# Score masks on ScalarE and GpSimd, and input loads issued one by one, in a fused attention and SwiGLU kernel

## The chip, the cores and the metric

The kernel runs on one core of one Trainium2 chip. The metric is the device time of one execution in microseconds. Five engines work side by side: TensorE multiplies matrices and writes to PSUM, VectorE (DVE) and ScalarE (ACT) compute elementwise and can read PSUM, GpSimd (POOL) computes elementwise in SBUF, and SyncE (SP) issues transfers. Each works through its own list of instructions and waits on semaphores of the others.

## The reference

Everything is float32. First a gated linear recurrence per batch row and head, then a feed-forward block over all tokens:

```python
batch, n_heads, seq, head_dim = (4, 8, 768, 48)      # d_model 384, d_ff 1536
f = 1.0 / (1.0 + np.exp(-f_logit))
for t in range(S):
    state = f[:, :, t, :, None] * state + np.einsum('bhd,bhe->bhde', k[:, :, t], v[:, :, t])
    y[:, :, t] = np.einsum('bhd,bhde->bhe', q[:, :, t], state)
x = y.transpose(0, 2, 1, 3).reshape(B * S, H * D)
g = x @ w_gate
out = (g / (1.0 + np.exp(-g)) * (x @ w_val)) @ w_out
```

## The kernel before

The sequence is cut into six chunks of 128 tokens, c = 0 to 5. A unit is one chunk of one batch row, written (c,b) here; in the code its number is u = 4c + b. The recurrence over a chunk becomes matrix work. With running products of the gates, k and q are scaled (`kT`, `qT`), the scores are `kT` times `qT` over the chunk's tokens, and a mask keeps the scores whose key is not later than the query. From them and from the decayed state comes `y`, and the state is carried to the next chunk. The feed-forward block then takes a whole chunk of all four batch rows (512 tokens) at once.

`attention(u)` is a generator. Each `yield` ends a step, and a table of times (`times`, line 873) says at which point of the running feed-forward block each step is written into the program. The steps of a unit from chunk 2 on are, in order: the sigmoid of f on ScalarE (L584); VectorE's transpose of f into `gates` (L593); its transpose of k (L601); a backward scan (L605); the product `kT` (L559); for the turned units, those of chunks 3 and 4, a transpose of `kT` into the room of k and four transfers through DRAM (L620 to L624); a forward scan (L631); the transpose of q (L635); the product `qT`; the scores (L651) and, where not turned, a transpose of `kT` on TensorE (`kt`, L655); the emptying of both (L659 to L667); then the decay of the state, `y`, and the state's update.

Inputs of chunks 2 to 5 land in `rooms["f"]`, `rooms["k"]` and `rooms["q"]`, one room for each input, in four transfers of 32 tokens each on SP's queue (L438 to L442). A room can be filled again only when it has been transposed. `load_after(u)` (L744) does it once per unit: after the transpose of q it issues the loads of f, q and k for unit u + 1. v has rooms of its own and is loaded elsewhere.

The scores of a unit fill two PSUM banks of 128x512, one for even heads and one for odd. `SCORES` (L863) names when they are written and where they go: "b" is a pool of three small-work banks, "A" and "o" are banks of the feed-forward block. "A" has two banks, "o" two and "B" one, and a bank given out again waits until the earlier content has been read. In chunks 3 to 5 the units of b = 1 and 2 use "o" at the start of a triple and b = 3 uses "A" in the down phase; b = 0 uses "b" in chunk 3 and "A" after that. In chunk 2 the order is b, o, A, A.

The feed-forward block of a chunk (`mlp_fifteen`, L946) has four triples of fifteen products and then a down phase. A product is a pair of 128x256 matmuls. Within a triple its products go into the banks A, B, o, A, B, o, A, B, c, A, B, c, A, B, A ("c" also takes an "o" bank). All products named A of one triple share one bank, and those named B too, so each is copied to SBUF by ScalarE (L997) before the next one writes. VectorE joins the copies with sums (L893, L896), ScalarE applies Silu (L1008), and VectorE multiplies (L944). Products are counted from one: the third goes into "o", the fourth into A again, the seventh into A once more.

Nothing is reordered behind this plan. `in_order` (L759) ties the instructions of each engine, GpSimd and SP included, to the order in which they were written:

```python
    in_order(mark, (mybir.EngineType.PE, mybir.EngineType.DVE, mybir.EngineType.Activation, mybir.EngineType.Pool, mybir.EngineType.SP))
```

GpSimd's list in this part holds only small memsets of `gates` (L639), the transfers that carry `yT` into `xT` (L702, ten for a unit), and some output transfers. The functions that the change touches, and what calls them:

Of the kernel before, what the change touches and what calls it, by code (L numbers as in the profile page):

```python
# [14 lines left out]
ALU = mybir.AluOpType  # L15
# [275 lines left out]
def short_path(ctx, tc, ident, least, judge, q, k, v, f_logit, moe_w_gate, moe_w_val, moe_w_out, out):  # L291
# [9 lines left out]
    nc = tc.nc  # L301
    B, H, S, D = q.shape
    C = 128
    NCH = S // C
    HP = H // 2
# [10 lines left out]
    SQUARES = 2  # L316
# [16 lines left out]
    causal = const.tile([128, C], FP32, tag="causal", name="causal")  # L333
    nc.gpsimd.memset(causal, 1.0)
    nc.gpsimd.affine_select(out=causal, in_=causal, compare_op=ALU.is_ge, fill=0.0, base=0,
                            pattern=[[1, C]], channel_multiplier=-1)
# [27 lines left out]
    def pairs(t, off=0):  # L364
        return t[:, off:off + HP * N1].rearrange("p (a t) -> p a t", t=N1)
# [23 lines left out]
    units = [(b, c) for c in range(NCH) for b in range(B)]  # L389
# [16 lines left out]
    def v_of(u):  # L406
        return vs[u % (NV if units[u][1] < SQUARES else NV // 2)]

    def squares(nm):
        return rooms[nm][:, Q:Q + HP * RUN].rearrange("t (a i e) -> t a i e", a=HP, i=NI)[:, :, :, 0:Q]  # L410

    def split_squares(nm):
        return squares(nm).rearrange("t a (j i) e -> t a j i e", j=2)

    def in_turn(t):

        return t.rearrange("p a (t i) -> p a i t", i=NI)

    def parted(t):

        return t.rearrange("p (j a t i) -> p a j i t", j=2, a=HP, i=NI // 2)

    def load(u, what="fkqv"):
        b, c = units[u]
        rows = slice(c * C, (c + 1) * C)
        inputs = dict(f=f_logit, k=k, q=q, v=v)
        for nm in "fkqv" if c < SQUARES else "fqkv":
            src = inputs[nm]  # L430
            if nm not in what:
                continue
            if nm == "v":
                dst = v_of(u)
            elif c < SQUARES:
                dst = raw[nm][u % NRAW]
            else:
                for n in range(4):  # L438
                    at = Q * (1 - n % 2)
                    nc.sync.dma_start(  # L440
                        out=rooms[nm][Q * n:Q * (n + 1), at:at + HP * RUN].rearrange("t (a e) -> t a e", a=HP),
                        in_=src[b, n // 2::2, rows, :].rearrange("a (t i) d -> t a (i d)", i=NI))  # L442
                continue
            nc.sync.dma_start(out=dst[:, :, 0:D], in_=src[b, :, rows, :].rearrange("h t d -> t h d"))
# [88 lines left out]
    def bank(name):  # L533
        return banks[-1].tile([128, 512], FP32, tag="a", name=name)
# [10 lines left out]
    def attention(u):  # L545
        b, c = units[u]
# [29 lines left out]
        def transposed(name, src):  # L576
            p = bank(name)
            for a in range(HP):
                nc.tensor.transpose(p[:, a * C:(a + 1) * C],
                                    src[:, 2 * a:2 * a + 2, :].rearrange("t r d -> t (r d)"), ident)  # L580
            return p.rearrange("p (a t) -> p a t", t=C)
# [6 lines left out]
        else:  # L588
            p = transposed("fTp", fr)
            nc.scalar.activation(pairs(gate)[:, :, 1:N1], p, AF.Copy if u in ahead else AF.Sigmoid)  # L590
        yield
        if c >= SQUARES:
            nc.vector.transpose(in_turn(pairs(gate)[:, :, 1:N1]), squares("f"))  # L593
        yield

        kT = att.tile([128, HP, C], FP32, tag="kT", name="kT")
        qT = att.tile([128, HP, C], FP32, tag="qT", name="qT", bufs=2)
        kp, qp = kT, qT
        if c >= SQUARES:
            kp = qT.rearrange("p a t -> p (a t)")  # L600
            nc.vector.transpose(parted(kp), split_squares("k"))  # L601
        yield

        n = HP * N1
# [7 lines left out]
            qp = transposed("qTp", qr)  # L612
        multiply(kT, kp, pairs(tail, 2)[:, :, 0:C])
        yield
        turned = SQUARES < c < NCH - 1
        if turned:


            beside = rooms["k"][:, 0:HP * C].rearrange("p (i m) -> p i m", i=NI)
            nc.vector.transpose(beside.rearrange("p i (a e) -> p a i e", e=Q), kT.rearrange("p a (i e) -> p a i e", e=Q))  # L620
            turn = turn_pool.tile([Q, NI, HP, NI, Q], FP32, tag="turn", name="turn")
            for r in range(NI):
                nc.sync.dma_start(out=turn[:, :, :, r, :].rearrange("t i a e -> t (i a) e"),
                                  in_=beside[Q * r:Q * (r + 1)].rearrange("t i (a e) -> t (i a) e", e=Q))  # L624
        yield

        if c >= SQUARES:
# [5 lines left out]
        if c >= SQUARES:  # L633
            qp = tail[:, 0:HP * C]
            nc.vector.transpose(parted(qp), split_squares("q"))  # L635
            load_after(u)
        yield
        multiply(qT, qp, pairs(gate)[:, :, 1:N1])
        nc.gpsimd.memset(pairs(gate)[:, :, 0:1], 0.0)  # L639
        if 0 < c < SQUARES:  # L640
            load_after(u)
        if c < SQUARES:
            decay()
        yield
# [1 line left out]
        A = att.tile([128, 2, HP, C], FP32, tag="A", name="A")  # L646
        sc = [score_bank(u) for _ in range(2)]
# [4 lines left out]
        if c < NCH - 1 and not turned:  # L652
            p = bank("kt")
# [9 lines left out]
            else:  # L663
                nc.scalar.copy(kt, p)
        for par in range(2):
            nc.vector.tensor_tensor(A[:, par], sc[par].rearrange("p (a t) -> p a t", t=C),  # L666
                                    causal.unsqueeze(1).broadcast_to((128, HP, C)), ALU.mult)  # L667
        yield
        if c >= SQUARES:
            decay()  # L670
# [4 lines left out]
        if c and b < B - 1:  # L675
# [20 lines left out]
            for h in range(H):  # L696
                a, par = h // 2, h % 2
                f = h * D
                while f < (h + 1) * D:
# [3 lines left out]
                                                                       in_=yT[r:r + n, par, a // 2 * C:(a // 2 + 1) * C])  # L703
# [25 lines left out]
        if c < NCH - 1:  # L729
            p = bank("dS")  # L730
# [10 lines left out]
            nc.vector.tensor_tensor(states[b], decayed[:, :, 0:D], dS, ALU.add)  # L741
        yield

    def load_after(u):  # L744

        w = u + (1 if units[u][1] >= SQUARES else 2)
        if w < len(units) and (units[w][1] >= SQUARES) == (w == u + 1):
            load(w, "fkqv" if units[w][1] < SQUARES or w == SQUARES * B else "fkq")

    def attention_steps(c):  # L750

        runs = [attention(c * B + b) for b in range(B)]
        parts = [3, 6, 3, 3]
        order = sorted((2 * b + s, b, n) for b in range(B) for s, n in enumerate(parts))
        return [lambda b=b, n=n: [next(runs[b]) for _ in range(n)] for _, b, n in order]
# [125 lines left out]
    def score_bank(u):  # L881
        b, c = units[u]
        kind = SCORES[c][b][1] if c >= SQUARES else "b"
        if kind == "b":
            return bank("sc")
        return {"o": banks_o, "A": banks_a}[kind].tile([128, 512], FP32, tag=kind, name="sc")
# [314 lines left out]
    mark = traced[-1]  # L1201
    keep_warm(5)
    first = [attention(b) for b in range(B)]
    done = [0] * B

# [83 lines left out]
    for c in range(2, NCH):  # L1289
        for b in range(B):  # L1290
            run = attention(c * B + b)
            waiting += [((c - 2) * whole + t, lambda run=run: next(run)) for t in times(c)[b]]
# [107 lines left out]
```

## Time and profile before

Three runs gave 608.85, 607.35 and 607.47 us; the median is 607.47. The profiled execution:

| | |
|---|---|
| its own time | 607.02 us |
| span from first to last instruction | 605.3 us |
| VectorE masks, L666, all chunks | 48 of 684 ns, 30.9 us |
| of these from chunk 2 on | 32 of 685 ns, 20.6 us as the union of their times |
| ScalarE copies 128x512 from "A" to `c`, L997 | 40 of 584 ns |
| ScalarE table loads from 144 us on | 22 of 1283 ns |
| GpSimd transfers `xT<-yT`, L702 | 120 of 509 ns |
| GpSimd select 128x128 at the start, L335 | 284 ns |
| loads of f, k and q into the rooms | 64 transfers each, 96 KB, 2.2 to 2.5 us to landing |

Busy time by stretch, one for each fifteen-product block (chunks 1 to 5), in us:

| stretch | length | TensorE | VectorE | ScalarE | GpSimd |
|---|---|---|---|---|---|
| 144 to 241 | 97 | 96.06 | 84.70 | 49.81 | 15.64 |
| 241 to 337 | 96 | 95.24 | 81.58 | 48.89 | 16.53 |
| 337 to 430 | 93 | 93.00 | 77.40 | 47.92 | 16.52 |
| 430 to 521 | 91 | 91.00 | 67.00 | 43.67 | 16.41 |
| 521 to 605 | 84 | 79.29 | 44.86 | 33.90 | 1.10 |

A line of the timeline has the start in us, the duration in us, the engine with its line in the code, the operation, what it writes and reads, the size, how many instructions were merged, and in brackets the idle time of the engine before it with what ended it. In TensorE's waits the columns are the total in us, the number of times and the longest. PE is TensorE's matmuls and PEld its weight loads. The busy time of TensorE is modelled to the end of a pipelined matmul, so a loss is best seen in the starts: two products in a row start 0.86 us apart. The attention units of chunk c run beside the block of chunk c - 1; 521 to 605 has none.

### The profile page before, as it was taken

The page shows a single profiled execution, that of the slowest core. Times are in us where ns is not written, and L with a number is a line of the kernel's source. Part 1 is how long each engine was busy: PE and PEld are TensorE (multiplying, and loading weights), DVE is VectorE, ACT ScalarE, POOL GpSimd, SP SyncE. Part 2 cuts the span into 40 slices and gives each one's busy share as a digit, 9 for nine tenths or more (in the row PEclk, how much of TensorE's full clock was granted, in tenths as well). Part 3 has the DMA queues.
Part 4 walks back from the last instruction along what each step waited for, and adds up shares of the span by engine and source line. Part 5 has one row for each costly group of instructions (what it writes and reads, how often), then busy time and mean ns, then how long its engine had stood idle before and what let it go on. Part 6 is the DMA issues. An engine that isn't in the chain of part 4 may idle for free.

```text
span 605.3 us, 10815 instructions
## 1 busy us (share of the span) xinstructions
PE 592.4 (98%) x4028; PEld 487.7 (81%) x4028; DVE 476.5 (79%) x825; ACT 292.5 (48%) x557; POOL 70.4 (12%) x175
## 2 busy tenths in 40 slices
PE   7899999999999999999999999999999999999996
PEld 5744545667888899878899988899988899988896
DVE  7999895968999977989995978995878982566741
ACT  3567662314876521476632376742276740366600
POOL 1000000000030050030330030330030321000000
PEclk9999999999999999999999999999999999999999
DMA  9999371014231144443345243244231100100001
GB/s 198 242 251 357 136 198 27 7 27 138 80 82 48 45 117 104 104 112 96 73 112 127 78 117 95 53 120 110 74 105 52 28 7 9 53 1 1 1 1 56
DMA packets 110299, 55.11 MB, mean 91 GB/s; under 512 B 72992, under 2 KB 102688, under 8 KB 110240
## 3 DMA queue, kind: packets, MB, share of 16 engines
q1 hardware_dynamic: 103872, 47.67, 30.0%
q0 software_dynamic: 4352, 3.94, 1.9%
q10 hardware_dynamic: 2016, 2.75, 1.2%
q8 instruction: 33, 0.54, 0.4%
q14 instruction: 26, 0.21, 0.1%
HBM read 44.56 MB, written 6.82 MB: 85 GB/s over the span
## 4 chain that ended last, share of the span: by engine, by line
PE 87%; DVE 9%; issue 1%; ACT 1%; DMA 1%; SPq 0%; DVEq 0%; ACTq 0%
PE o L1091 19%; PE A L992 15%; PE B L992 12%; PE gate L790 5%; PE val L790 5%; PE c L992 5%; PE o L992 5%; PE sc L651 4%; PE o L1154 3%; PE o L813 3%; PE y L691 2%; PE y L712 2%; PE dS L732 2%; PE y L687 1%; DVE c L896 1%
## 5 line engine op out<-in xcount | busy, mean ns | idle before, releaser
L702 POOL DMA_DIRECT2D xT<-yT x120 | 60.1, 509 | 54.2 <-ACT yT L695 51.7
L992 PE MATMUL A<-xs,w_both 128*128 128x256 f32 x240 | 62.3, 382 | 0.8 <-ACT c L997 0.8
L1091 PE MATMUL o<-w_out,h 128*128 128x192 f32 x360 | 62.0, 327 | 0.5 <-DVE h L944 0.5
L1091 PEld LDWEIGHTS o<-w_out,h 128*128 128x128 f32 x360 | 58.7, 190 | 1.7 <-DVE h L944 0.8
L997 ACT COPY c<-A 128x512 f32<-128x512 f32 x40 | 23.3, 584 | 57.7 <-PE A L992 57.7
L997 ACT COPY aside<-A 128x512 f32<-128x512 f32 x60 | 35.1, 585 | 33.1 <-PE A L992 33.0
L992 PEld LDWEIGHTS A<-xs,w_both 128*128 128x128 f32 x240 | 44.8, 190 | 7.7 <-ACT c L997 1.2
L893 DVE TENSOR_TENSOR c<-c,aside 128x512 f32<-128x512 f32 x60 | 41.1, 685 | 12.4 <-ACT aside L997 10.8
L944 DVE TENSOR_TENSOR h<-h,c 128x256 f32<-128x256 f32 x100 | 40.5, 413 | 7.8 <-ACT h L1008 7.6
L666 DVE TENSOR_TENSOR A<-sc,causal 128x512 f32<-128x512 f32 x48 | 30.9, 684 | 17.6 <-PE sc L651 17.6
L1008 ACT ACTIVATE h<-c 128x256 f32<-128x256 f32 x100 | 39.2, 416 | 7.8 <-DVE c L893 5.6
L896 DVE TENSOR_TENSOR c<-c,aside 128x512 f32<-128x512 f32 x60 | 40.9, 682 | 2.5 <-ACT aside L997 2.5
L1091 PE MATMUL o<-ws,h 128*128 128x192 f32 x240 | 41.5, 328 | 0.2 <-DVE A L666 0.2
L992 PE MATMUL B<-xs,w_both 128*128 128x256 f32 x160 | 41.3, 380 | 0.1
L992 PE MATMUL A<-xs,extra 128*128 128x256 f32 x160 | 41.3, 380 | 0.0
L992 PE MATMUL c<-xT,w_both 128*128 128x256 f32 x160 | 41.2, 380 | 0.1
L992 PE MATMUL B<-xT,extra 128*128 128x256 f32 x160 | 41.1, 379 | 0.0
L639 POOL MEMSET gates<- 128x4 f32 x24 | 3.0, 123 | 326.3 <-DVE qT L559 321.2
L997 ACT COPY aside<-B 128x512 f32<-128x512 f32 x60 | 35.1, 586 | 9.6 <-PE B L992 7.0
L1091 PEld LDWEIGHTS o<-ws,h 128*128 128x128 f32 x240 | 39.1, 190 | 0.8 <-DVE A L666 0.4
L893 DVE TENSOR_TENSOR c<-c,o 128x384 f32<-128x384 f32 x15 | 8.3, 552 | 36.0 <-PE o L1091 36.0
L896 DVE TENSOR_TENSOR c<-o,c 128x512 f32<-128x512 f32 x40 | 27.3, 684 | 10.6 <-ACT h L1008 6.2
(142 smaller groups left out, 1199.2 us busy)
## 6 DMA issues: line engine op xcount, KB each, us to landing
fsquares<-in_f_logit_dram SPq DMA_DIRECT2D x64, 96.0 KB, 2.5
qsquares<-in_q_dram SPq DMA_DIRECT2D x64, 96.0 KB, 2.2
ksquares<-in_k_dram SPq DMA_DIRECT2D x64, 96.0 KB, 2.2
v<-in_v_dram SPq DMA_DIRECT2D x24, 192.0 KB, 2.8
w<-in_moe_w_gate_dram SPq DMA_DIRECT2D x6, 768.0 KB, 6.3
w<-in_moe_w_val_dram SPq DMA_DIRECT2D x6, 768.0 KB, 6.0
w<-in_moe_w_out_dram SPq DMA_DIRECT2D x6, 768.0 KB, 5.0
out_dram<-ob ACTq DMA_DIRECT2D x14, 192.0 KB, 2.5
```

Of the source, the lines that this page charges most:

```text
L651: nc.tensor.matmul(sc[par][:, a * C:(a + 1) * C], lhsT=kT[r, a, :], rhs=qT[r, a, :], start=True, stop=True)
L666: nc.vector.tensor_tensor(A[:, par], sc[par].rearrange("p (a t) -> p a t", t=C), causal.unsqueeze(1).broadcast_to((128, HP, C)), ALU.mult)
L702: (nc.gpsimd if c >= SQUARES else nc.sync).dma_start(out=xT[c][f % 128:f % 128 + n, f // 128, b * C:(b + 1) * C], in_=yT[r:r + n, par, a / ...
L790: nc.tensor.matmul(p, lhsT=w[:, j, i, :], rhs=xT[c][:, i, :], start=(i == 0), stop=(i == KT - 1))
L813: nc.tensor.matmul(p, lhsT=hidden_tile(h, n // 2)[:, n % 2 * 2 + b // 2, b % 2 * C:(b % 2 + 1) * C], rhs=w_out[:, j, :], start=(n == 0), s ...
L893: nc.vector.tensor_tensor(dst, a, b, ALU.add)
L896: nc.vector.tensor_tensor(dst, a, b, ALU.subtract)
L944: lagging.append(lambda: f(*args))
L992: nc.tensor.matmul(p[name][:, n, :], lhsT=weights_of[a][:, n, j, :], rhs=tokens[b], start=fresh and n == 0, stop=True, skip_group_check=True)
L997: nc.scalar.copy(t, p[name])
L1008: nc.scalar.activation(dst, src[:, 0, :], AF.Silu)
L1091: nc.tensor.matmul(p[:, n, :], lhsT=lhsTs[j][:, n * C:(n + 1) * C], rhs=rhs[:, j, :], start=first and j == order[0] and n == 0, stop=j == ...
```

## The change

For chunks 2 to 5 the masking of the scores is split. ScalarE copies each score bank into `A`, and GpSimd then sets to zero in place what lies on the wrong side of the diagonal. The steps stay where they were written. Chunks 0 and 1 keep the multiplication by `causal` on VectorE.

`load_after` now takes the names of what to load for the next unit and is called three times: for f behind f's transpose, for k behind k's transpose (in turned units behind the four transfers out of k's room), and for q behind q's transpose. The loads of chunk 1 keep their rule, written out in place.

```diff
@@ -591,14 +591,18 @@
         yield
         if c >= SQUARES:
             nc.vector.transpose(in_turn(pairs(gate)[:, :, 1:N1]), squares("f"))
-        yield
-
+            load_after(u, "f")
+        yield
+
+        turned = SQUARES < c < NCH - 1
         kT = att.tile([128, HP, C], FP32, tag="kT", name="kT")
         qT = att.tile([128, HP, C], FP32, tag="qT", name="qT", bufs=2)
         kp, qp = kT, qT
         if c >= SQUARES:
             kp = qT.rearrange("p a t -> p (a t)")
             nc.vector.transpose(parted(kp), split_squares("k"))
+            if not turned:
+                load_after(u, "k")
         yield
 
         n = HP * N1
@@ -612,7 +616,6 @@
             qp = transposed("qTp", qr)
         multiply(kT, kp, pairs(tail, 2)[:, :, 0:C])
         yield
-        turned = SQUARES < c < NCH - 1
         if turned:
 
 
@@ -622,6 +625,7 @@
             for r in range(NI):
                 nc.sync.dma_start(out=turn[:, :, :, r, :].rearrange("t i a e -> t (i a) e"),
                                   in_=beside[Q * r:Q * (r + 1)].rearrange("t i (a e) -> t (i a) e", e=Q))
+            load_after(u, "k")
         yield
 
         if c >= SQUARES:
@@ -633,12 +637,12 @@
         if c >= SQUARES:
             qp = tail[:, 0:HP * C]
             nc.vector.transpose(parted(qp), split_squares("q"))
-            load_after(u)
+            load_after(u, "qv" if c < SQUARES else "q")
         yield
         multiply(qT, qp, pairs(gate)[:, :, 1:N1])
         nc.gpsimd.memset(pairs(gate)[:, :, 0:1], 0.0)
-        if 0 < c < SQUARES:
-            load_after(u)
+        if 0 < c < SQUARES and u + 2 < SQUARES * B:
+            load(u + 2)
         if c < SQUARES:
             decay()
         yield
@@ -663,8 +667,13 @@
             else:
                 nc.scalar.copy(kt, p)
         for par in range(2):
-            nc.vector.tensor_tensor(A[:, par], sc[par].rearrange("p (a t) -> p a t", t=C),
-                                    causal.unsqueeze(1).broadcast_to((128, HP, C)), ALU.mult)
+            p = sc[par].rearrange("p (a t) -> p a t", t=C)
+            if c >= SQUARES:
+                nc.scalar.copy(A[:, par], p)
+                nc.gpsimd.affine_select(out=A[:, par], in_=A[:, par], compare_op=ALU.is_ge, fill=0.0, base=0,
+                                        pattern=[[0, HP], [1, C]], channel_multiplier=-1)
+            else:
+                nc.vector.tensor_tensor(A[:, par], p, causal.unsqueeze(1).broadcast_to((128, HP, C)), ALU.mult)
         yield
         if c >= SQUARES:
             decay()
@@ -741,11 +750,10 @@
             nc.vector.tensor_tensor(states[b], decayed[:, :, 0:D], dS, ALU.add)
         yield
 
-    def load_after(u):
-
-        w = u + (1 if units[u][1] >= SQUARES else 2)
-        if w < len(units) and (units[w][1] >= SQUARES) == (w == u + 1):
-            load(w, "fkqv" if units[w][1] < SQUARES or w == SQUARES * B else "fkq")
+    def load_after(u, what):
+
+        if u + 1 < len(units):
+            load(u + 1, what)
 
     def attention_steps(c):
 
```

In program order ScalarE's new copies follow directly on these instructions, up to the next one of the list:

| unit | ScalarE's order around the two new copies |
|---|---|
| (2,0) | `c<-A`, `c<-B`, `kt`, **both**, table load, Silu, `c<-A` |
| (2,1) | `c<-A`, `kt`, **both**, `c<-B`, table load, Silu, `c<-A` |
| (2,2), (2,3) | `yT` twice, `kt`, **both** |
| (3,0) | `c<-A`, `c<-B`, `c<-A`, **both**, `aside<-B` |
| (3,1), (3,2), (4,1), (4,2), (5,1), (5,2) | `yT` twice, `c<-A`, **both**, `c<-B`, table load, Silu, `c<-A` |
| (3,3), (4,3), (5,3) | `yT` twice, **both**, `diagonal` |
| (4,0), (5,0) | `xT`, **both**, output transfers |

## Prediction

> **What bounds the kernel now.** I read the totals and the chain of waits first, then TensorE's waits, then the order of time around every place where the change puts an instruction. Chunks count from 0 here, as in the code, so the third chunk is c=2, and (c,b) is one unit. The page and TensorE's waits:
>
> ```profile
> span 605.3 us, 10815 instructions
> PE 592.4 (98%) x4028; PEld 487.7 (81%) x4028; DVE 476.5 (79%) x825; ACT 292.5 (48%) x557; POOL 70.4 (12%) x175
> ...
> PE 87%; DVE 9%; issue 1%; ACT 1%; DMA 1%; SPq 0%; DVEq 0%; ACTq 0%
> ```
>
> ```profile
> PE A L992 <- ACT c L997: 0.8, 1, 0.8
> ...
> PE o L1091 <- DVE h L944: 0.5, 1, 0.5
> ...
> PE o L1091 <- DVE A L666: 0.2, 1, 0.2
> ```
>
> TensorE sets the end: 98% busy, 87% of the chain. VectorE's 79% is no bound by itself. Every edit acts after 144 us, where the first fifteen-product block starts. There TensorE starts a product every 0.86 us, and a longer step between two starts is lost time. I find five: the second product of a triple starts at 189.99 instead of 189.70 (0.29), another at 196.38 (0.25), the down phase at 205.97 (0.70), 223.03 (0.18) and 262.46 (0.93), in all 2.35 us. From 265 us to the end there is none. So the change can win little more than 2.35 us, 0.4%, however much VectorE is relieved, while anything that holds TensorE costs in full.
>
> The last of these losses belongs to the loads:
>
> ```profile
> 257.75 1.16 PE L651 MATMUL sc<-qT,kT 48*128 48x128 f32 x16
> ...
> 258.94 1.29 DVE L666 TENSOR_TENSOR A<-sc,causal 128x512 f32<-128x512 f32 x2 [0.51 <-PE sc L651]
> ...
> 259.46 1.28 ACT L584 ACT_TABLE_LOAD   x1 [3.70 <-DMA fsquares<-in_f_logit_dram]
> ...
> 262.46 1.13 PE L992 MATMUL A<-xs,w_both 128*128 128x256 f32 x4 [0.76 <-ACT c L997]
> ```
>
> ScalarE stood 3.70 us before the sigmoid of (3,2) because f's squares had not landed; the copy of the first product queued behind it, and the next product into that bank waited.
>
> **What the Trainium skill says.** "PSUM — Partial Sum Buffer", section "Engine vs sequencer instructions": ScalarE, VectorE and GpSimd queues are strict FIFO, and matmuls start in program order. The trace agrees: the copy at 262 us stood behind a sigmoid that it does not need. "GPSIMD Engine Reference", section 3.1: a one-input loop of 512 elements took 769 ns; no trace here shows a select of that size. "SBUF — State Buffer", section "SBUF: two separate sides": a VectorE instruction with two SBUF inputs and a GpSimd instruction that reads SBUF exclude each other for a whole instruction. Before, GpSimd reads no SBUF but for two selects at the start, so the trace does not show it.
>
> **The change part by part.** The plan of positions and banks is untouched; only who empties the score banks changes, and each engine keeps its written order.
>
> *VectorE loses* the two masks of each of 16 units: 32 x 0.685 = 21.9 us busy, 1.29 us per unit. From 265 us on TensorE loses nothing to VectorE, so there it brings nothing. The losses at 189.99, 196.38 and 205.97 hang on VectorE's backlog (weight sums of 1.35 us at 187 and 194 among them). But the masks of (2,1) lie at 175.36, and VectorE then works up to TensorE's third product (starts at 178.61, 0.11 after that ended at 178.50). What is gained earlier is waited away there. I take 0; bound -1.25 us.
>
> *ScalarE gains* two copies of 128x512 from PSUM per unit. The row of the same shape has 584 ns, and copies in a row start 0.48 to 0.49 apart. What counts is what stands behind them:
>
> ```profile
> 353.38 1.29 DVE L666 TENSOR_TENSOR A<-sc,causal 128x512 f32<-128x512 f32 x2 [2.85 <-PE sc L651]
> ...
> 354.44 0.59 ACT L997 COPY c<-A 128x512 f32<-128x512 f32 x1 [1.80 <-PE A L992]
> ...
> 355.11 1.03 PE L992 MATMUL o<-xT,w_both 128*128 128x256 f32 x4
> 355.31 0.59 ACT L997 COPY c<-B 128x512 f32<-128x512 f32 x1 [0.28 <-PE B L992]
> ...
> 355.91 1.28 ACT L1008 ACT_TABLE_LOAD   x1
> ```
>
> (4,1) has its scores in both "o" banks, and the third product takes the first of them again. VectorE freed it at 354.07, long before 355.11. In the new order the copies stand behind `c<-A`, although the scores lie ready from 353.35: first copy 354.93 to 355.52, TensorE 0.05 later (as at 262.41/262.46), so the third product starts at 355.57: 0.46 us lost. After such a stop the following product comes 0.10 late as well (262.46 to 263.43 is 0.97 instead of 0.86; at 189.99 the same). The later bank waits still hold: `c<-A` of the fourth product would end at 358.71 instead of 358.10, and the seventh product, itself now after 359, needs it. So 0.56 us per unit. The same sum at (3,2), (4,2), (5,1), (5,2) (`c<-A` ends 291.27, 384.57, 447.88, 476.96; third product 291.34, 384.64, 447.96, 477.04) gives 0.46 to 0.47 each. Five units: 2.8 us.
>
> (2,1) is such a unit too, with the `kt` copy in front:
>
> ```profile
> 176.81 0.59 ACT L997 COPY c<-A 128x512 f32<-128x512 f32 x1 [2.55 <-PE A L992]
> ...
> 177.30 0.59 ACT L664 COPY kt<-kt 128x512 f32<-128x512 f32 x1
> ...
> 177.48 1.03 PE L992 MATMUL o<-xT,w_both 128*128 128x256 f32 x4
> ```
>
> `kt` ends at 177.89, the first score copy at 178.38, so the third product starts at 178.43 instead of 177.48: 0.95 + 0.10 = 1.05 us.
>
> (2,0) has its scores in other banks, but ScalarE is full there: copy, copy, `kt`, table load, Silu, and `c<-A` ends at 163.94 with the seventh product starting at 163.99 on that very copy. Two copies ahead of the table load push all by 2 x 0.49: 0.97 us.
>
> (2,3): the scores hold both "A" banks and the down phase's next sum takes the first at once:
>
> ```profile
> 222.28 1.29 DVE L666 TENSOR_TENSOR A<-sc,causal 128x512 f32<-128x512 f32 x2 [2.20 <-PE sc L651]
> 222.93 0.59 ACT L664 COPY kt<-kt 128x512 f32<-128x512 f32 x1 [1.80 <-PE kt L655]
> 223.03 1.44 PEld L1091 LDWEIGHTS o<-ws,h 128*128 128x128 f32 x9 [0.43 <-DVE A L666]
> ```
>
> Today VectorE frees it at 222.97. After: `kt` to 223.51, first copy 223.41 to 224.00, TensorE at 224.05: 1.02 us. The remaining units, (2,2), (3,0), (3,3), (4,0), (4,3), (5,0), (5,3), cost nothing: ScalarE waits around them and their banks come round 4 us later or more; (3,0) has the least cover, the copy for the eighth product ending at 248.21 against 248.54.
>
> *GpSimd gains* 32 selects. The select of 128x128 took 284 ns. Four times its elements at the same fixed part is about 0.54 us with the memset rows' slope (205 ns for 128 elements, 123 for 4), and 1.14 at most; I take the page's 0.77. They queue behind a unit's ten `xT` DMAs (5 us). Tightest is (2,2): DMAs until about 215.5, two selects to 217.1, the `y` matmul reading A at 219.61. It would wait only above 2 us per select. Price 0. If selects and VectorE's two-input instructions block each other, VectorE loses up to 2 x 0.77 per unit and gets 1.29 back; where it has no slack, between (2,1)'s selects at about 180 and 190, that is up to +1.5 us. I take 0, range 0 to 1.5.
>
> *Loads.* f is fetched behind f's own transpose, k behind its own (turned units: behind the turn DMAs that read k's room), q last. For (3,2) the f DMAs go out at about 244.7, when its predecessor's transpose ends, instead of 255.16; with 2.5 us to land they are there by 250, before ScalarE is ready at 255.77. On SP the `kt` load of (3,0) moves behind them, to about 246.6, needed at 257.20: covered. The 3.70 us wait goes, and TensorE's 0.93 with its 0.10. But then (3,1), whose score copies stand there, meets the "o" bank wait like the others, 0.46 and 0.10. Net -0.47 us. Elsewhere no load is late for TensorE: 0.
>
> **Sum.** 0.97 + 1.05 + 1.02 + 2.80 - 0.47 = +5.4 us. On the profiled execution's own 607.02 us (span 605.3 and 1.7 around it) that is 612.4 us, +0.9%. The median of the three runs is 607.47, 0.45 above the profiled one; on it the sum would be 612.9. I keep 612.4.
>
> **Rivals.**
> 1. *Bank waits and ScalarE's queue, as summed*: 612.4. For: each place has its start times; against: VectorE's slack may repay some. Chance 0.55.
> 2. *VectorE's relief repays in chunk 2*: the stops at 190, 196 and 206 (1.24 and three times 0.10) disappear: 610.9. For: VectorE is 98% busy from 180 to 210 us (29.4 of 30); against: the wait at 178.61. Chance 0.13.
> 3. *GpSimd and VectorE block each other*: +1.5 around 190, 613.9, and more if it recurs. Chance 0.14.
> 4. *The other side: VectorE's backlog is the true limit.* All five losses with their restarts go (2.35 + 0.4) and none of the new waits appears: 604.3. It decides if the copies release the "o" banks before the third product, that is, if they ran in ScalarE's 1.8 us gap ahead of `c<-A`. The written order speaks against it. Chance 0.09.
> 5. *Gains and waits cancel*: half the new waits (2.9) against the losses: 607 to 608. Chance 0.09. If f's load does not come in time, (3,1) keeps its loss: 612.9, inside case 1.
>
> **How the numbers follow.** About 0.3%, 1.8 us, can be told from no change. Slower: cases 1 to 3, 0.82; same: case 5, 0.09; faster: case 4, 0.09. The range takes cases 1 to 3 with their unknown costs, from 1.24 repaid plus a few copies that hide better, 609.5, to 1.5 of blocking plus second-order delays, 614.8.
>
> **What would show it.** TensorE's waits should name ScalarE's score copy ahead of `o` products in the third product of (2,1), (3,1), (3,2), (4,1), (4,2), (5,1) and (5,2), 0.4 to 0.5 us each and twice that at the first; a wait of about 1 us in the down phase of (2,3) and one near 165 us; none on f's DMA. VectorE's durations of two-input rows should stay at 0.68. I am wrong if the third products start on time, if VectorE's rows grow, or if a `y` matmul waits for GpSimd.

## The result, and the profile after

The changed kernel took 612.07 us (median of six runs, 612.0 to 612.94) against 607.42 for the kernel before (six runs, 607.22 to 608.85). The ratio is 1.0073, interval 1.006 to 1.0086: slower by 0.7%. The profiled execution took 612.16 us, its span 610.4, against 607.02 and 605.3. The forecast was 612.4, a sum of 5.4 us on top of the profiled execution before.

The page of the changed kernel, with its totals and its chain of waits:

```profile
span 610.4 us, 10917 instructions
...
PE 594.6 (97%) x4028; PEld 488.1 (80%) x4028; DVE 461.9 (76%) x793; ACT 308.2 (50%) x589; POOL 97.3 (16%) x207
...
PE 89%; DVE 7%; ACT 2%; issue 1%; ACTq 0%; DVEq 0%
```

VectorE did become lighter: 476.5 to 461.9 us. ScalarE gained 15.7 us and GpSimd 26.9, and both still idle half of the time or more. Read by busy shares, the change relieves the second busiest engine with two idle ones. Yet the end came 5 us later. TensorE's waits in the changed kernel (total in us, times, longest) say why:

```profile
PE o L1000 <- ACT A L672: 2.6, 7, 0.8
...
PE o L1099 <- ACT A L672: 1.2, 1, 1.2
PE A L1000 <- ACT c L1005: 0.9, 1, 0.9
...
PE o L1099 <- DVE h L952: 0.5, 1, 0.5
```

The first two rows are new. ScalarE's score copy (L672) now holds TensorE eight times: seven third products and one sum of the down phase. The third row looks like the one shown of before, `PE A L992 <- ACT c L997` with 0.8, and is another event: there it was the product at 262 us behind f's load, now it is the seventh product of (2,0) near 165 us, whose copy is late because two score copies were put ahead of it. A figure of this list is the idle time before the instruction and is not the loss itself. So I set the starts of all matmuls of both traces side by side; the loss is what the distance grows by. It is 0.12 us at 144 us, where the first block begins. It then grows by 0.975 us in (2,0), by 1.06 in (2,1), by 1.03 in (2,3), and by 0.57 at each of six more, and shrinks by 1.13 at the wait for f. The last of TensorE's products starts 5.43 us late, so 5.31 come from the region of the change. (The span grew by 5.1: what follows the last product was about 0.3 shorter. Single executions of one kernel differ by more than that, so it is the shifts of the starts, and not the totals, that are set against the terms of the prediction.)

One of the six, in the timeline of the changed kernel:

```profile
357.61 0.59 ACT L1005 COPY c<-A 128x512 f32<-128x512 f32 x1 [2.16 <-PE A L1000]
358.09 1.08 ACT L672 COPY A<-sc 128x512 f32<-128x512 f32 x2
358.73 0.73 PEld L1000 LDWEIGHTS o<-xT,w_both 128*128 128x128 f32 x4 [0.70 <-ACT A L672]
...
359.05 0.62 ACT L1005 COPY c<-B 128x512 f32<-128x512 f32 x1
```

ScalarE stood idle for 2.16 us, and for the last 1.1 of them the scores lay ready (their matmuls end at 356.51). It waited for the first product, because the copy `c<-A` is written ahead of the score copies, and only then emptied the "o" bank. The third product starts 0.05 us after the first of the two copies ends (358.09 + 0.59 = 358.68).

### The profile page after: what moved, and what is told of

The parts are those of the page before. It is cut to its first block, busy times and chain, and to the rows that moved or that the text cites. A ratio compares the mean times of both kernels' runs of the same rounds, so it can differ in the third digit from the quotient of the medians.

```text
span 610.4 us, 10917 instructions
## 1 busy us (share of the span) xinstructions
PE 594.6 (97%) x4028; PEld 488.1 (80%) x4028; DVE 461.9 (76%) x793; ACT 308.2 (50%) x589; POOL 97.3 (16%) x207
## 4 chain that ended last, share of the span: by engine, by line
PE 89%; DVE 7%; ACT 2%; issue 1%; ACTq 0%; DVEq 0%
PE o L1099 19%; PE A L1000 16%; PE B L1000 12%; PE o L1000 6%; PE c L1000 5%; PE gate L798 5%; PE val L798 5%; PE sc L655 4%; PE o L1162 3%; PE o L821 3%; PE y L700 2%; PE y L721 2%; PE dS L741 2%; PE y L696 1%; PE kt L659 1%
## 5 line engine op out<-in xcount | busy, mean ns | idle before, releaser
L1000 PEld LDWEIGHTS A<-xs,extra 128*128 128x128 f32 x160 | 30.3, 190 | 5.4 <-ACT c L1005 1.3
```

Of the source, the lines that this page charges most:

```text
L1000: nc.tensor.matmul(p[name][:, n, :], lhsT=weights_of[a][:, n, j, :], rhs=tokens[b], start=fresh and n == 0, stop=True, skip_group_check=True)
```

## The experiments

Each expectation was written before its kernel ran. All ratios are to the kernel before, run on the same chip.

**The loads alone.** The masks stay VectorE's multiplication; the loads are split as in the change. This edit and the next are shown against the changed kernel, shortened (`...`).

```diff
         for par in range(2):
-            p = sc[par].rearrange("p (a t) -> p a t", t=C)
-            if c >= SQUARES:
-                nc.scalar.copy(A[:, par], p)
-                nc.gpsimd.affine_select(out=A[:, par], in_=A[:, par], ...)
-            else:
-                nc.vector.tensor_tensor(A[:, par], p, ...causal..., ALU.mult)
+            nc.vector.tensor_tensor(A[:, par], sc[par]..., ...causal..., ALU.mult)
```

> The masks stay on VectorE, the loads are issued one by one as in the change. If ScalarE's queue and the bank waits are the whole cost, none of them is here and only the late f of (3,2) goes: TensorE starts its products after 265 us 1.13 us earlier than before (0.93 for the wait, 0.20 for the two restarts behind it), so about 606.3 us, 0.998 of before. If the reordered loads themselves cost something (the kt loads now stand behind f's loads on SP), it is no faster than before, 607.4 or more.

Measured: 605.93 us (605.62 to 608.17), ratio 0.9978, interval 0.9968 to 0.9987. TensorE's starts shift at one place only, by -0.93 and two restarts of -0.10, where f was late; its last product moves by -1.11. ScalarE's waits for f's loads, before:

```profile
ACT fsquares L584 <- DMA fsquares<-in_f_logit_dram: 10.4, 3, 5.2
...
ACT L584 <- DMA fsquares<-in_f_logit_dram: 4.1, 2, 3.7
```

and in the changed kernel:

```profile
ACT fsquares L584 <- DMA fsquares<-in_f_logit_dram: 4.0, 1, 4.0
```

Five waits of 14.5 us in all became one of 4.0 (3.8 with the loads alone), which lies at 138 us, ahead of the region of the change. Of the 10.5 us only one wait, the 3.7 of (3,2), had held TensorE. So the loads are the good part of the change, and they are worth 1.1 us.

**The masks alone.** The loads are issued as before (the remarks behind `#` are not in the code).

```diff
-            load_after(u, "f")       # behind f's transpose
-                load_after(u, "k")   # behind k's transpose, or the turn
-            load_after(u, "q")
+            load_after(u)            # all three behind q's transpose
```

> The masks move to ScalarE and GpSimd, the loads stay as before. My theory: the same losses at (2,0), (2,1), (2,3) and the five o-bank units (0.98, 1.06, 1.03 and 5 x 0.57), but at (3,1) ScalarE is late by f's wait and the score copy comes behind that: the third product waits from 260.67 to about 262.94, 2.37 us with its restart, in place of the 1.13 us of before. Sum +7.1 us: 614.6, 1.0117 of before. If the split loads and the masks were independent, this would be after plus 1.13 us, 613.2. If VectorE's relief pays for anything, less than either.

Measured: 615.8 us (614.61 to 616.93), ratio 1.0147, interval 1.0128 to 1.0166; TensorE's last product 8.37 us late. The new stops are those of the change, with two differences. First, the third product of (3,1) loses 2.97 us, not the 2.27 expected. The timeline of this kernel:

```profile
263.21 1.28 ACT L584 ACT_TABLE_LOAD   x1 [4.05 <-DMA fsquares<-in_f_logit_dram]
...
265.56 0.60 ACT L1002 COPY c<-A 128x512 f32<-128x512 f32 x1
...
266.03 1.10 ACT L668 COPY A<-sc 128x512 f32<-128x512 f32 x2
...
266.70 1.13 PE L997 MATMUL o<-xT,w_both 128*128 128x256 f32 x4 [2.81 <-ACT A L668]
```

The sigmoid of the next unit waits for f, and behind it stand `c<-A`, the score copies, and with them TensorE. A load that did not stand ahead of the mask in the kernel before now does, in ScalarE's queue. The extra 0.7 has two halves. f's transfers begin to issue 3.39 us later than in the kernel before (258.55 against 255.16), while TensorE was 3.04 late by then; and from there to ScalarE's table load for the sigmoid it takes 4.66 us instead of 4.30. The four took 3.31 us to issue instead of 2.05; why, stays open. The two parts of the change are not independent: splitting the loads is worth 1.1 us by itself and 3.1 (8.37 against 5.31) where the masks are on ScalarE.

Second, there are two stops that neither the kernel before nor the changed one has, 0.14 us at 276 and 0.47 at 371. What stands out ahead of the larger one is an instruction seven microseconds earlier:

```profile
364.75 1.23 POOL L669 TENSOR_SCALAR_AFFINE_SELECT A<-A 128x512 f32<-128x512 f32 x2
...
364.88 1.64 DVE L898 TENSOR_TENSOR c<-c,aside 128x512 f32<-128x512 f32 x1 [0.54 <-ACT aside L1002]
...
371.31 0.92 PE L997 MATMUL B<-xT,extra 128*128 128x256 f32 x3 [0.31 <-ACT aside L1002]
```

A VectorE sum of two SBUF tiles, 0.69 us elsewhere, takes 1.64 us and ends within 0.6 us of the two selects beside it. That looks like the exclusion named in the prediction, here with a price; the link from this sum to the stop at 371 was not tested by itself.

**The `kt` copy behind the score copies.** Against the changed kernel, the block that copies `kt` is moved behind the loop that empties the score banks (the transposed tile is renamed `pk`).

```diff
-        if c < NCH - 1:
-            kt = att.tile(...)
-            ...
-                nc.scalar.copy(kt, p)
         for par in range(2):
             ...
+        if c < NCH - 1:
+            kt = att.tile(...)
+            ...
+                nc.scalar.copy(kt, pk)
```

> The change, with the kt copy written behind the two score copies. My theory: (2,3) loses nothing (its first score copy ends near 222.9 on the clock of before, ahead of 223.03), gain 1.03 us against after; at (2,1) the first score copy is one copy earlier, gain 0.49. So 612.1 - 1.5 = 610.6 us. If those two stops came from something else, such as GpSimd or the transposes of kT, it stays at 612.1.

Measured: 610.9 us (610.78 to 610.97), ratio 1.0062, interval 1.0045 to 1.0079; TensorE's last product 4.22 us late instead of 5.43. In (2,1) the third product's loss falls from 0.95 to 0.46, what all other units of this kind lose. In (2,3) the new stop goes altogether. Two small ones appear instead, 0.12 with its restart at the seventh product of (2,1) and 0.19 at 190 us; together 0.4, they account for the 0.3 above the expectation. The price of a stop is what stands ahead of the copy, instruction by instruction.

**The score copies right behind the scores.** In addition, the table of times puts the masking step directly behind the score matmuls, so that it is written ahead of `c<-A`.

```diff
-        masks = {"b": 2, "o": 0.9, "A": 1.5}
+        masks = {"b": 0.03, "o": 0.03, "A": 0.03}
```

> As kt_behind, and the emptying of the scores is written right behind the score matmuls in every unit, so that in ScalarE's list both copies stand ahead of the copy of the next product. All work of the change is still done. My theory: ScalarE stands idle at just these points (1.7 to 2.6 us in seven units), so all eight new stops vanish and only the gain of f's load is left: 606.3 us, 0.998 of before. If VectorE's backlog had been the limit in chunk 2, up to 1.2 us more is won, 605.1. If GpSimd's selects blocking VectorE are part of the cost, or ScalarE's 18.7 us of additional work as such, it stays clearly above before, 609 or more.

Measured: 605.74 us (605.56 to 607.04), ratio 0.9978, interval 0.997 to 0.9986. The stops on ScalarE's score copies are gone, and (2,0)'s too; what is left beside the gain at f is -0.18 in (2,0), where a small stop of the kernel before (0.08, with its restart) goes, +0.34 at 190 us and -0.05 at 223. The place of the first example, (4,1), in this kernel's timeline:

```profile
351.16 1.16 PE L655 MATMUL sc<-qT,kT 48*128 48x128 f32 x16
...
352.41 1.07 ACT L666 COPY A<-sc 128x512 f32<-128x512 f32 x2 [1.15 <-PE sc L655]
...
353.42 0.59 ACT L1005 COPY c<-A 128x512 f32<-128x512 f32 x1
...
354.08 1.03 PE L1000 MATMUL o<-xT,w_both 128*128 128x256 f32 x4
```

The copies fill the time in which ScalarE had waited, and the third product starts without a wait. This shows that the new stops came from neither the copies nor the selects as work, which are all still there, but from their place in ScalarE's order. And it shows that the masks off VectorE are worth nothing as they stand: the loads alone reach the same ratio. In this kernel's timeline VectorE stands idle until it can read the third product of (2,1):

```profile
178.43 0.69 DVE L904 TENSOR_TENSOR c<-o,c 128x512 f32<-128x512 f32 x1 [2.31 <-PE o L1000]
...
179.24 1.23 POOL L667 TENSOR_SCALAR_AFFINE_SELECT A<-A 128x512 f32<-128x512 f32 x2
...
180.00 0.76 DVE L952 TENSOR_TENSOR h<-h,c 128x256 f32<-128x256 f32 x1
...
190.14 1.13 PE L1000 MATMUL B<-xs,w_both 128*128 128x256 f32 x4 [0.46 <-ACT aside L1005]
```

The freed time lies in the 2.31 us in brackets. The 0.76 two lines on is a product that takes 0.42 elsewhere, beside the selects.

**Without the selects, and with each twice.** Both start from the last kernel. Without the selects the scores stay unmasked, so this kernel leaves out a part of the work and serves for the times alone.

```diff
                 nc.scalar.copy(A[:, par], p)
-                nc.gpsimd.affine_select(out=A[:, par], ...)
```

> As at_once without GpSimd's 32 selects, so the scores are copied and not masked. If selects and VectorE's instructions with two SBUF inputs shut each other out, VectorE's scans go back from 1249 and 1341 ns to 1.22 us as before, and TensorE's stop of 0.63 us at 190 (product starts at 188.65 and 190.14, 1.49 apart instead of 0.86) shrinks to the 0.29 of before or less. Time about 605.5 us, too near at_once to tell. If the long rows have another cause, they and the stop stay.

```diff
-                nc.gpsimd.affine_select(out=A[:, par], ...)
+                for _ in range(2):
+                    nc.gpsimd.affine_select(out=A[:, par], ...)
```

> As at_once with every select run twice in a row (the second changes nothing), so GpSimd's additional work doubles. Exclusion theory: VectorE's two-input rows grow further (scan means above 1.30 us), the stop at 190 grows by 0.3 to 0.8 us, and the other tight places of chunk 2 at 196 and 206 may grow; 606.0 to 607.0 us. If GpSimd's work is free as long as it is off TensorE's path, 605.7 us as at_once and the same stop at 190.

Measured: 606.08 us without (one run, so no more than a hint), 607.5 with each twice (607.06 to 609.24; ratio 0.9994, interval 0.9985 to 1.0003). The times differ too little to carry this; the places do. Without the selects the same product on VectorE and the same start on TensorE:

```profile
180.00 0.42 DVE L950 TENSOR_TENSOR h<-h,c 128x256 f32<-128x256 f32 x1
...
189.79 1.13 PE L998 MATMUL B<-xs,w_both 128*128 128x256 f32 x4
```

0.76 becomes 0.42 and 190.14 becomes 189.79: the same 0.34 to 0.35 us at both ends, ten microseconds apart, since VectorE has next to no idle time between them (9.97 us busy of the 10 from 180 to 190). With each select twice TensorE's wait at this place is 1.0 us instead of 0.5, and from 144 us on its last product loses 1.3 us to the kernel with one: 0.5 here, the rest in steps of 0.1 to 0.2 in later blocks. VectorE's scans, the groups of 16 in the profile from 144 us on, without the selects:

```profile
L609 DVE TENSOR_TENSOR_SCAN tails<-gates,floor 128x516 f32<-128x516 f32 x16 | 19.5, 1221 | 0.0
L635 DVE TENSOR_TENSOR_SCAN gates<-gates,start 128x516 f32<-128x516 f32 x16 | 19.5, 1219 | 0.0
```

and in the changed kernel:

```profile
L635 DVE TENSOR_TENSOR_SCAN gates<-gates,start 128x516 f32<-128x516 f32 x16 | 20.4, 1274 | 0.0
L609 DVE TENSOR_TENSOR_SCAN tails<-gates,floor 128x516 f32<-128x516 f32 x16 | 20.4, 1274 | 0.0
```

The blocking is real in the change too. A scan took 0.05 us more on the mean, because single ones beside two selects took 1.63 to 1.68. VectorE's busy time fell by only 14.6 us there, though masks of 20.6 had left it; without the selects it is 457.1 us, against 463.6 with them in the kernel with the copies right behind the scores. In these runs it held TensorE only where VectorE had no slack.

**VectorE's relief used.** If the 2.31 us of idle time are the reason why the relief brings nothing, then sums moved into them should bring it out. From the kernel with the copies right behind the scores, the places of three sums over `w_out` are moved. One was there already; two more now stand ahead of the sum that reads the third product of (2,1):

```diff
-    DOWN_SUMS_AT = (28, 34, 38, 48)
+    DOWN_SUMS_AT = (26, 28, 28, 48)
```

> As at_once, with three of the four weight sums for the down phase (1.3 us each on VectorE) written where the two masks of (2,1) used to be: VectorE waits 2.31 us there for TensorE's third product. If VectorE's backlog between 180 and 206 us is what stops TensorE at 190, 196 and 206, the relief now counts: those stops and their restarts (0.63, 0.25, 0.70 and 0.3 together) go, 603.9 us, 0.9943 of before. If not, 605.7 as at_once.

Measured: 603.83 us (603.67 to 604.52), ratio 0.9937, interval 0.9917 to 0.9958. The three sums and the wait for the third product, in this kernel's timeline (the first, at 173.66, is left out):

```profile
175.59 1.35 DVE L904 TENSOR_TENSOR ws<-w_out,ws 128x1152 f32<-128x1152 f32 x1
...
176.86 1.35 DVE L904 TENSOR_TENSOR w_out<-w_out 128x1152 f32<-128x1152 f32 x1
...
178.46 0.69 DVE L904 TENSOR_TENSOR c<-o,c 128x512 f32<-128x512 f32 x1 [0.25 <-PE o L1000]
```

2.31 us idle have become 0.25, and the stops at 190, 196 and 206 are gone, by 0.63, 0.24 and 0.71 and their restarts. To see whether this needs the masks off VectorE, the same move was made in the kernel with the loads alone.

> As loads_only (masks on VectorE) with the same three sums moved. It tells whether the room that the moved masks leave is needed. VectorE would then reach the sum after the third product about 1.2 us late, and has 2.7 us less to do after 187. If that delay is absorbed, the stops at 190, 196 and 206 go here too and it is as fast as sums_early, 604.3; if the room is needed, TensorE gets a new stop of up to 1.2 us between 180 and 190 and it gains less than 0.6 us on loads_only's 605.9.

Measured: 604.8 us (604.54 to 605.03), ratio 0.995, interval 0.993 to 0.9969. Those three stops go here as well, but for 0.05 at 190; two small ones of 0.07 appear near 187. So most of the gain is that of the moved sums, which the kernel before could probably have had too (the sums without the split loads were not run). Between the two kernels lie 1.0 us, and their runs do not overlap, but the intervals of the ratios do. In the two traces 0.43 us of the difference had already arisen by 144 us, where the programs do not yet differ; counted from there, TensorE's last product comes 2.91 us earlier than before with the masks moved and 2.42 without. So the masks on ScalarE and GpSimd add about 0.5 us: 0.26 around 190, 0.18 in (2,0), 0.05 at 223. This rests on one trace of each. The version with all of it is the fastest of this study and beats both kernels.

## Why the prediction was right, step by step

| step | predicted, us | measured, us |
|---|---|---|
| (2,0): two copies ahead of the copy for the seventh product | 0.97 | 0.975 |
| (2,1): third product behind `c<-A`, `kt`, first copy | 0.95 + 0.10 | 0.953 + 0.104 |
| (2,3): down phase behind `kt` and first copy | 1.02 | 1.028 |
| (3,2), (4,1), (4,2), (5,1), (5,2): third product | 5 x 0.56 | 5 x 0.567 |
| (3,1): bank wait against f's wait | 0.56 - 1.03 | 0.567 - 1.132 |
| VectorE's relief | 0 (bound -1.25) | 0 (-0.03 at 190) |
| exclusion of GpSimd and VectorE | 0 (to 1.5) | 0 |
| sum, from 144 us on | 5.37 | 5.31 |

*The bank waits.* Every one came where it was put and with its size. What made these terms exact is that nothing in them had to be guessed. The order in ScalarE's queue is written, the durations of the copies stand in rows of the same shape, and the next user of each bank is named in the code. The Trainium skill, "PSUM — Partial Sum Buffer", section "Engine vs sequencer instructions", calls the queues strict FIFO (first in, first out). This agrees with the 1.1 us for which ScalarE stood idle ahead of 357.61 with the scores ready, and with the stops that vanished when only the place of the copies was changed.

In (2,0) the lines show the chain from the copies to the product, in the timeline of the changed kernel:

```profile
161.74 1.09 ACT L672 COPY A<-sc 128x512 f32<-128x512 f32 x2
...
162.85 1.28 ACT L1016 ACT_TABLE_LOAD   x1
...
164.47 0.57 ACT L1005 COPY c<-A 128x512 f32<-128x512 f32 x1
...
165.09 1.13 PE L1000 MATMUL A<-xs,extra 128*128 128x256 f32 x4 [0.89 <-ACT c L1005]
```

The scores here are in banks that nobody wants soon. The price comes from the queue alone: the seventh product waits for a copy that stands behind the two new ones.

*f's wait.* The gain was put 0.10 too small: a second restart went with it. It is the only place off by more than 0.01. It explains more than the whole 0.06 by which the sum is off; the others gave 0.04 back. The prediction's list of TensorE's losses also missed a sixth, 0.08 us with its restart at 163.99; that is why the new stop of (2,0), at the same product, brought no restart of its own.

*VectorE's relief.* Zero is confirmed by the stops at 192.11, 198.51 and 208.09 of the changed kernel, which kept their 0.26, 0.25 and 0.71 us. Nor did the blocking hide a gain there: without the selects, at 190, 196 and 206, these three lose 0.26, 0.25 and 0.71 as well. The reason given, that what is gained is waited away ahead of the third product, is what the last two experiments bear out. In the changed kernel VectorE idles there for 3.37 us:

```profile
180.52 1.23 POOL L673 TENSOR_SCALAR_AFFINE_SELECT A<-A 128x512 f32<-128x512 f32 x2
180.76 0.69 DVE L904 TENSOR_TENSOR c<-o,c 128x512 f32<-128x512 f32 x1 [3.37 <-PE o L1000]
...
182.32 0.41 DVE L952 TENSOR_TENSOR h<-h,c 128x256 f32<-128x256 f32 x1
```

*The exclusion.* Zero was right in the sum, but by luck: the prediction took it without a reason, and a sign that it had named for being wrong came true, VectorE's rows grew. The lines above show why it cost nothing in the critical stretch. The selects end at 181.75, and the product that they could have stretched starts at 182.32 and takes its 0.41. In both this kernel and the one with the copies right behind the scores, the selects start when GpSimd's ten transfers of `yT` end (180.52 and 179.24), not when the copies do. But here the stop of the third product, 1.06 us with its restart, had pushed the product on VectorE past them: it starts 1.80 us behind the first select, against 0.76 there, where the overlap came and 0.34 us with it. So the change was spared this cost by its own stop. The Trainium skill, "SBUF — State Buffer", section "SBUF: two separate sides", says that a VectorE instruction with two SBUF inputs and a GpSimd instruction that reads SBUF block each other for a whole instruction. The 1.64 us sum beside two selects and the return to 0.42 without them agree.

*The selects.* The prediction took 0.77 us for each, the figure that it cites for a one-input loop of that length. They took 0.65 in the median, so the figure was too high here, and 1.58 at the longest; no instruction of TensorE waits for GpSimd anywhere in this trace. The tile view of `A` (min, median, max in ns):

```profile
L672 ACT COPY A<-sc x32: 586/592/616, 161.7 to 503.1; 128x512 f32<-128x512 f32 x32
L673 POOL TENSOR_SCALAR_AFFINE_SELECT A<-A x32: 632/648/1582, 162.4 to 507.3; 128x512 f32<-128x512 f32 x32
```

*The rivals.* That VectorE's backlog is the true limit falls with the stops that stayed. But its condition, copies that run ahead of `c<-A`, was the right one for their disappearance: when it was made true, all new waits went. Its other half, that the five old losses go with it, did not happen then. f's went with the loads; those at 190, 196 and 206 went only when the sums were moved; of the 0.18 at 223 only 0.05 went.

*The total.* That 612.4 lies within 0.4 us of the measured median is in part luck. The sum was put on the profiled execution, whose 607.02 lies 0.4 below the median of before; on a median the forecast would have been 612.9, as the prediction says. Between the medians the loss is 4.65, 0.75 less than the sum. What confirms the prediction is the list of places, not the total.

## What to carry to other kernels

When the emptying of a shared PSUM bank moves to another engine, price it by what stands ahead of it in that engine's queue and by who wants the bank next; the busy share of the new engine tells neither. If the move is wanted, write the copy directly behind the matmuls that fill the bank and ahead of anything that waits. Relieving an engine off the critical path paid here only when other work was moved into the hole that this left ahead of its next wait.

## What the runs showed of the hardware

A VectorE instruction with two inputs in SBUF took, beside GpSimd selects, up to 1.64 us instead of 0.69, and 0.76 instead of 0.42; a select of 128x512 took 0.63 to 0.65 us for the most part, and up to 1.58 beside VectorE. At 190 us the delay reached TensorE by 0.35 us, and with each select twice by 0.9: the step between the two starts there is 1.12 us without selects, 1.49 with one and 2.01 with two.

Nearly every stop of TensorE on a semaphore cost a further 0.104 us, with the same size for stops of 0.25 and of 0.95 us: the seven new stops of third products made 0.7 us of it. The traces show it as a longer step from the start of the stopped product to the next (0.97 instead of 0.86), all of it between the first two matmuls behind the stop (0.32 instead of 0.22), and do not show what it is.
